# First head pair of a hashed attention kernel: four tiles of one head in turn, the second head's operands made later and elsewhere

## The chip, the cores and the metric

The kernel runs on one core of one Trainium2 chip. Its engines run in parallel, each through its own list of instructions in order: TensorE (PE, with its weight loads as PEld), VectorE (DVE), ScalarE (ACT), GpSimd (POOL) and SyncE (SP), which here only issues transfers. The metric is the device time of one execution in microseconds (us), lower is better; the median of several runs is given.

## The reference

Two stages, batch 4, 8 heads of 64, 768 positions. The first is attention in which a query sees only the keys of its own hash bucket; the bucket is six sign bits of a projection.

```python
q_bits = (np.einsum('bhsd,dk->bhsk', q, proj) > 0).astype(np.int64)
k_bits = (np.einsum('bhsd,dk->bhsk', k, proj) > 0).astype(np.int64)
mask = q_bucket[:, :, :, None] == k_bucket[:, :, None, :]
scores = np.where(mask, scale * np.matmul(q, k.transpose(0, 1, 3, 2)), -1000000000.0)
attn = np.exp(scores - np.max(scores, axis=-1, keepdims=True))
attn = attn / (np.sum(attn, axis=-1, keepdims=True) + 1e-09)
x = np.matmul(attn, v)                      # heads side by side: (4, 768, 512)
h = np.maximum(x @ w_in, 0.0)               # (4, 768, 1024)
gate = 1.0 / (1.0 + np.exp(-conv_out))      # conv_out: three taps conv_w along the positions of h
out = (h * gate) @ w_out
```

The weights and the taps come as 64-bit floats and are decoded on the chip.

## The kernel before, in words

**Pairs and units.** The 32 heads are worked in 16 pairs of two heads (`Pair`). A pair has 12 units (`Unit`): one tile of 128 queries of one head each, against all 768 keys. Units are numbered through the program, 0 to 191; pair 0 has units 0 to 11, pair 1 units 12 to 23. `Q1`, `K1`, `Q2` and `K2` are a pair's operands (named Q, K, q and k in the profile, since buffer numbers are left out): q and k are split into a high part (rounded to the fast matmul type) and the rest, and 12 rows at partitions 64 to 76 of `Q2` and `K2` carry the hash bits, so that a mismatch of one bit adds a large negative number to the score. The products `s` of a unit are four matmuls, two of `Q1` with `K1` over 128 rows and two of `Q2` with `K2` over 96 rows (L284). Rows 76 to 96 must be zero for that.

**One loop iteration** i puts on the engines: the products of unit i; its row maximum on VectorE with a copy out of PSUM (L295); for unit i - 4 the transposes on TensorE (L315) and the copy of the result to SBUF on ScalarE (L322, tile `at`); the exponential of unit i on ScalarE (L302); the normalisation of unit i - 1 on GpSimd (L310). The last product of unit i waits for the normalisation of unit i - 4. After four units of a block of 256 queries their product with the values follows (`values`, L330, 24 matmuls), at the next i with i % 4 = 1. Four PSUM slots of two banks go round (`slot`).

**The preparation** of pair p + 1 runs inside pair p (`prepare`): at k = 1 of pair p's units it begins and takes seven iterations, one step each. GpSimd makes the high part `hi` of head 0 (L201), four transfers of SyncE's queue bring it to its places (L204); two steps later GpSimd subtracts (L206) and two transfers follow (L208), and TensorE hashes both heads (L216); then GpSimd scales the bits (L221) and eight small transfers bring them to `K2` and `Q2` (L225); then head 1 as head 0. At k = 8 the load of pair p + 2's input `R` is issued (L188), at k = 10 the load of pair p + 1's values (L195).

**Pair 0** cannot be prepared inside an earlier pair. `prepare_now` computes its operands on the engines at once, without transfers: hashes of both heads on TensorE (L244), then for each head the high parts (L250 to L253), the low part of q (L254), the bits out of the hash (L258), the low part of k (L259), and the bits to their four places, two on ScalarE (L263) and two on GpSimd (L265). It is a generator: the first part runs ahead of the loop, the rest at i = 0 and i = 2. At i = 2 it also clears rows 64 to 96 of the second pair of `K2` and `Q2` buffers from a zero tile (L267, L268), which was filled at L78.

**The order** of every engine's list is the order in which the program issues the instructions; a tile's reader waits for its writer by semaphore, and transfers of SyncE's queue are issued in program order too. Before the loop SyncE loads pair 0's input, one head each (L186), and pair 1's (L188). The decoding of the three taps (`decode_taps`) starts at i = 3, one step per iteration; of the weights (`split_weights`) at i = 9. ScalarE's queue fetches one raw weight block of 512 KB at every i with i % 8 = 5 (L171).

Of the kernel before, what the change touches and what calls it, by code (L numbers as in the profile page):

```python
# [15 lines left out]
NB = 6  # L16
# [25 lines left out]
def lsh_attention_conv_ffn(ctx, tc, qk, v, hw, w_in, conv_w, w_out, consts, ident_in, out):  # L42
# [34 lines left out]
    zero = ring(wp, 4, [P, 2, S], F32, "big", "zero")  # L77
    nc.vector.memset(zero[64:96], 0.0)  # L78
# [97 lines left out]
    class Pair:  # L176
        def __init__(self, b, p):
            self.b, self.p, self.nm = b, p, f"{b}_{p}"
# [57 lines left out]
        def prepare_now(self):  # L236

            nm = self.nm
            hps = []
            for h in range(2):  # L240
                hps.append(slot(f"hash{nm}_{h}")[:, 0, :HS])
                for g in range(4):
                    c, half = 32 * (1 + g // 2), g % 2
                    nc.tensor.matmul(hps[h][32 * g:32 * g + 32], hw_sb[:, c:c + 32],  # L244
                                     self.R[:, h, half * HS:(half + 1) * HS].bitcast(F32),
                                     start=True, stop=True, tile_position=(0, 32 * g))
            for h in range(2):
                R = self.R[:, h].bitcast(F32)
                Q1, Q2, K1, K2 = (t[:, h] for t in (self.Q1, self.Q2, self.K1, self.K2))
# [4 lines left out]
                nc.vector.tensor_tensor(Q1[64:], R[:64], Q1[:64].bitcast(F32), ALU.subtract)  # L254
# [3 lines left out]
                nc.vector.tensor_scalar(bits, hps[h], 0.0, cst[:, 2:3], ALU.is_gt, ALU.subtract)  # L258
                nc.vector.tensor_tensor(K2[:64], R[64:], K1[64:].bitcast(F32), ALU.subtract)  # L259
                for g, dst in enumerate((K2, K2, Q2, Q2)):  # L260
                    p, dst = slice(32 * g, 32 * g + 32), dst[64:96, g % 2 * HS:(g % 2 + 1) * HS]
                    if g % 2 == 0:
                        nc.scalar.activation(dst, bits[p], AF.Copy, scale=cst[p, 3:4])  # L263
# [297 lines left out]
```

## Time and profile before

| | |
|---|---|
| median of 3 runs | 713.14 us (712.91 to 715.44) |
| profiled execution | 711.98 us, of which the span of instructions 710.2 us |
| mean granted clock of TensorE | 0.995 |
| TensorE busy | 693.9 us (98% of the span) |
| VectorE, ScalarE, GpSimd busy | 511.8, 484.5, 449.8 us |
| start of the first matmul | 4.43 us |

How to read it: the profile is one execution. Its page gives busy times and groups of instructions; the timeline gives the start and length of single instructions, or of a few alike in a row (x4), with the idle time before them and what ended it in brackets; SPq and ACTq are transfers at their issue. A stretch (a line that begins with A:B) gives the busy time of each engine in it, the granted clock of TensorE as a share of full speed, and the transfers' rate. A matmul of the program stands in the profile as two records where its type needs two passes, so that the hash of a head, four matmuls, is eight.

### The profile page before, as it was taken

How to read it: one execution, taken by the hardware profiler on the slowest of the kernel's cores; microseconds unless marked ns; L12 is line 12 of the kernel's file. 1: busy time of each engine (PE TensorE's matmuls, PEld its weight loads, DVE VectorE, ACT ScalarE, POOL GpSimd, SP SyncE). 2: the span in 40 equal slices, each digit the busy share in tenths (PEclk: the TensorE clock that was granted, in tenths of full speed). 3: DMA queues.
4: the chain of work that ended last, by engine and by line, in shares of the span. 5: the costliest groups of instructions: out<-in, count | busy, mean ns of one | idle time of the engine just before them, and what ended most of it. 6: DMA issues, size and time to landing. Idle time of an engine off the chain costs nothing.

```text
span 710.2 us, 13439 instructions
## 1 busy us (share of the span) xinstructions
PE 693.9 (98%) x4552; PEld 581.4 (82%) x4552; DVE 511.8 (72%) x1303; ACT 484.5 (68%) x892; POOL 449.8 (63%) x422
## 2 busy tenths in 40 slices
PE   5999999999999999999999999999999999999997
PEld 2777877877877877877877888898999899999996
DVE  7878888888888887887666664576667666755563
ACT  5878888878888887878777776455545554545453
POOL 5877887987888887889777642463256226622221
PEclk8999999999999999999999999999999999999999
DMA  3667757757758648748647402001201210101011
GB/s 127 153 197 214 181 155 210 197 149 214 194 145 230 193 130 226 209 110 234 188 114 220 113 27 93 8 30 48 102 0 45 89 46 1 45 1 44 1 46 44
DMA packets 39573, 84.77 MB, mean 119 GB/s; under 512 B 6960, under 2 KB 14672, under 8 KB 39504
## 3 DMA queue, kind: packets, MB, share of 16 engines
q1 hardware_dynamic: 36912, 75.47, 37.6%
q10 hardware_dynamic: 2592, 8.44, 3.8%
q8 instruction: 36, 0.59, 0.4%
q14 instruction: 33, 0.27, 0.1%
HBM read 33.70 MB, written 12.58 MB: 65 GB/s over the span
## 4 chain that ended last, share of the span: by engine, by line
PE 92%; DVE 2%; ACT 2%; DMA 1%; issue 1%; POOL 0%; POOLq 0%; ACTq 0%; SPq 0%
PE h L353 19%; PE s L284 19%; PE o L399 19%; PE v L330 17%; PE t L315 16%; PE hash L216 2%; ACT e L302 1%; DVE e L295 1%; DMA k<-R 1%; ACT at L322 1%; DMA R<-in_qk 0%; DVE Q L254 0%; DVE k L259 0%; DVE Q L252 0%; POOL e L310 0%
## 5 line engine op out<-in xcount | busy, mean ns | idle before, releaser
L310 POOL TENSOR_SCALAR e<-e,st 128x768 f32<-128x768 f32 x192 | 184.4, 963 | 64.7 <-DVE st L309 31.7
L322 ACT COPY at<-t 128x768 f32<-128x768 f32 x192 | 152.2, 793 | 67.7 <-PE t L315 67.6
L295 DVE TENSOR_SCALAR_CACHE_REDUCE e<-s 128x768 f32<-128x768 f32 x192 | 182.5, 950 | 22.0 <-PE s L284 14.4
L302 ACT ACTIVATE e<-e,st 128x768 f32<-128x768 f32 x192 | 181.1, 943 | 6.7 <-DVE st L299 4.7
L372 POOL TENSOR_TENSOR g<-ht,g 128x384 fp32r<-128x384 f32 x64 | 69.9, 1091 | 164.8 <-ACT g L371 132.0
L362 DVE SCALAR_TENSOR_TENSOR ht<-ht,cw 128x384 f32<-128x384 f32 (+1 forms) x128 | 119.0, 930 | 68.8 <-ACT ht L360 63.3
L315 PE MATMUL t<-ident,e 128*128 128x128 f32 x1152 | 157.2, 272 | 0.0
L353 PE MATMUL h<-x,wi 128*128 128x386 f32 x768 | 146.3, 339 | 1.3 <-ACT ht L358 1.3
L399 PE MATMUL o<-wo,g 128*128 128x512 f32 x576 | 143.4, 394 | 0.0
L315 PEld LDWEIGHTS t<-ident,e 128*128 128x128 f32 x1152 | 137.6, 140 | 6.8 <-DVE bits L219 0.2
L353 PEld LDWEIGHTS h<-x,wi 128*128 128x128 f32 x768 | 136.6, 188 | 7.5 <-ACT ht L358 1.7
L330 PE MATMUL v<-at,v 128*64 128x256 f32 x1152 | 134.9, 383 | 0.0
L399 PEld LDWEIGHTS o<-wo,g 128*128 128x128 f32 x576 | 107.3, 188 | 20.2
L284 PE MATMUL s<-K,Q 128*128 128x384 f32 x384 | 116.2, 384 | 3.6 <-POOL K L250 1.2
L330 PEld LDWEIGHTS v<-at,v 128*64 128x64 f32 x1152 | 78.3, 137 | 43.0 <-DVE st L309 4.7
L284 PE MATMUL s<-k,q 96*128 96x384 f32 x384 | 99.9, 341 | 2.7 <-DVE e L295 1.8
L365 ACT ACTIVATE ht<-ht 128x384 f32<-128x384 f32 x64 | 33.6, 526 | 97.7 <-DVE ht L362 97.7
L284 PEld LDWEIGHTS s<-K,Q 128*128 128x128 f32 x384 | 58.5, 192 | 33.6 <-ACT e L302 19.5
L284 PEld LDWEIGHTS s<-k,q 96*128 96x128 f32 x384 | 70.0, 190 | 4.8 <-ACT q L263 3.1
L366 DVE TENSOR_TENSOR ht<-ht 128x384 f32<-128x384 f32 x64 | 46.6, 728 | 33.7 <-ACT ht L365 33.7
L306 DVE TENSOR_SCALAR st<-st 128x1 f32<-128x1 f32 x192 | 29.2, 152 | 35.9 <-ACT e L302 30.7
L206 POOL TENSOR_TENSOR R<-R,hi 128x768 fp32r<-128x768 f32 x30 | 54.9, 1829 | 0.0
(65 smaller groups left out, 534.4 us busy)
## 6 DMA issues: line engine op xcount, KB each, us to landing
R<-in_qk SPq DMA_DIRECT2D x15, 768.0 KB
K<-hi SPq DMA_DIRECT2D x60, 192.0 KB
v<-in_v SPq DMA_DIRECT2D x16, 384.0 KB
xd<-x SPq DMA_DIRECT2D x48, 128.0 KB
x<-xd SPq DMA_DIRECT2D x16, 384.0 KB
out<-osb SPq DMA_DIRECT2D x24, 256.0 KB
Q<-hi SPq DMA_DIRECT2D x30, 192.0 KB
q<-hi SPq DMA_DIRECT2D x30, 192.0 KB
```

The lines of the kernel that those rows point to most:

```text
L206: nc.gpsimd.tensor_tensor(lo, R, hi.bitcast(F32), ALU.subtract)
L284: mm = nc.tensor.matmul(self.sp[:, half, :HS], A[:, h, qs], C[:, h, half * HS:(half + 1) * HS], start=(kk == 0), stop=(kk == 1))
L295: nc.vector.tensor_scalar(self.e.rearrange("p (a b) -> p a b", a=2), self.sp[:, :, :HS], MASKED, None, ALU.max, ALU.max, accum_out=self.st ...
L302: nc.scalar.activation(self.e, self.e, AF.Exp, bias=self.st[:, 1:2], scale=SCALE, accum_out=self.st[:, 2:3])
L310: self.norm = nc.gpsimd.tensor_scalar(self.e, self.e, self.st[:, 3:4], 0.0, ALU.mult, ALU.add)
L315: nc.tensor.transpose(self.tp[:, c // 3, c % 3 * P:(c % 3 + 1) * P], self.e[:, c * P:(c + 1) * P], ident)
L322: nc.scalar.copy(pr.at[self.h][:, :, :, self.tq * P:(self.tq + 1) * P], self.tp[:, :, :3 * P].rearrange("p j (c q) -> p j c q", c=3))
L330: nc.tensor.matmul(av[h * D:(h + 1) * D, :QB], pr.v[:, c, h, :], ats[h][:, c // 3, c % 3, :], start=(c == 0), stop=(c == NCK - 1), tile_po ...
L353: nc.tensor.matmul(hp[:, :HW], w, x[:, c0:c0 + HW], start=(n == 0), stop=(n == 3 * NCC - 1))
L362: nc.vector.scalar_tensor_tensor(t[:, a:z], ht[:, o + k - 1 + a:o + k - 1 + z], cw[:, f, k:k + 1], t[:, a:z], ALU.mult, ALU.add)
L372: nc.gpsimd.tensor_tensor(g[:, 1, :], t, g[:, 0, :].bitcast(F32), ALU.subtract)
L399: nc.tensor.matmul(op, l, r, start=(f == 0 and i == 0), stop=(f == NFC - 1 and i == 2))
```

## The change

All of it is at the start, but for the rows of the second products and the place of the taps.

- Pair 0 takes its units in another order: tiles 0 to 3 of head 0, then tiles 0 to 3 of head 1, then tiles 4 and 5 of either head. Before, it was tiles 0 and 1 of head 0, tiles 0 and 1 of head 1, and so on. Head 1 is first used by unit 4 instead of unit 2.
- `prepare_now` makes head 0's operands and head 1's high parts first. Head 1's `Q1` high part moves from VectorE to ScalarE and its low part from VectorE to GpSimd. Head 1's hash comes behind the products of unit 0, and its bits and low key behind those of unit 1.
- The products over `Q2` and `K2` take 76 rows instead of 96 (`NR`), and the zero tile, its filling and the two copies from it go.
- The preparation of pair 1 begins at k = 3 of pair 0's units instead of k = 1. The load of `R` for pair 2 stays at k = 8. In all later pairs it begins at k = 1 as before.
- The first block's values of pair 0 follow at i = 11 instead of 9, by a list instead of one variable; `at` tiles are taken per block and head.
- The taps are decoded from i = 152 on (unit 152 is in pair 12, counted from 0) instead of i = 3.

```diff
-    zero = ring(wp, 4, [P, 2, S], F32, "big", "zero")
-    nc.vector.memset(zero[64:96], 0.0)
+    NR = 64 + 2 * NB
...
         def prepare_now(self):
...
+            def hashes(h):
+                hp = slot(f"hash{nm}_{h}")[:, 0, :HS]
                 for g in range(4):
                     c, half = 32 * (1 + g // 2), g % 2
+                    nc.tensor.matmul(hp[32 * g:32 * g + 32], hw_sb[:, c:c + 32], R[h][:, half * HS:(half + 1) * HS],
                                      start=True, stop=True, tile_position=(0, 32 * g))
-            for h in range(2):
-                nc.gpsimd.tensor_scalar(K1[64:], R[64:], 1.0, 0.0, ALU.mult, ALU.add)
-                nc.scalar.copy(K1[:64], R[64:])
-                nc.vector.tensor_copy(Q1[:64], R[:64])
-                nc.scalar.copy(Q2[:64], R[:64])
-                nc.vector.tensor_tensor(Q1[64:], R[:64], Q1[:64].bitcast(F32), ALU.subtract)
-                if h == 1:
-                    yield
-                bits = ring(wp, 5, [P, WC], I32, "wl", f"bits{nm}_{h}").bitcast(F32)[:, :HS]
-                nc.vector.tensor_scalar(bits, hps[h], 0.0, cst[:, 2:3], ALU.is_gt, ALU.subtract)
-                nc.vector.tensor_tensor(K2[:64], R[64:], K1[64:].bitcast(F32), ALU.subtract)
...
+            def key(h):
+                nc.gpsimd.tensor_scalar(K1[h][64:], R[h][64:], 1.0, 0.0, ALU.mult, ALU.add)
+                nc.scalar.copy(K1[h][:64], R[h][64:])
...
+            hp = hashes(0)
+            key(0)
+            nc.vector.tensor_copy(Q1[0][:64], R[0][:64])
+            nc.scalar.copy(Q2[0][:64], R[0][:64])
+            nc.vector.tensor_tensor(Q1[0][64:], R[0][:64], Q1[0][:64].bitcast(F32), ALU.subtract)
+            t = bits(0, hp)
+            low_key(0)
+            key(1)
+            place(0, t)
+            nc.scalar.copy(Q2[1][:64], R[1][:64])
+            nc.scalar.copy(Q1[1][:64], R[1][:64])
+            yield
+            hp = hashes(1)
+            nc.gpsimd.tensor_tensor(Q1[1][64:], R[1][:64], Q1[1][:64].bitcast(F32), ALU.subtract)
+            yield
+            t = bits(1, hp)
+            low_key(1)
+            place(1, t)
-            yield
-            nc.vector.tensor_copy(K2s[1][64:96], zero[64:96])
-            nc.vector.tensor_copy(Q2s[1][64:96], zero[64:96])
...
-            for kk, (A, C) in enumerate(((pr.Q1, pr.K1), (pr.Q2, pr.K2))):
+            for kk, (A, C) in enumerate(((pr.Q1, pr.K1), (pr.Q2[:NR], pr.K2[:NR]))):
...
+    first_order = [(t, h) for ts in (range(4), range(4, NCK)) for h in range(2) for t in ts]
+    units = [Unit(pr, t, h) for pr in pairs for t, h in (first_order if pr is pairs[0] else order)]
...
-        if i in (0, 2):
+        if i in (0, 1):
             next(first, None)
-        if u and k == PREP and pi + 1 < len(pairs):
+        if u and k == (PREP if pi else 3) and pi + 1 < len(pairs):
             prep[0] = pairs[pi + 1].prepare()
         next(prep[0], None)
-        if av and (i % 4 == 1 or i >= n + LAG):
-            out_x = values(*av)
-            av = None
+        if av and (i >= av[0][0] + 2 or i >= n + LAG):
+            out_x = values(*av.pop(0)[1:])
         if burst:
-            av = w.pair, w.qb, w.pair.at
+            av.append((i, w.pair, w.qb))
...
-        if i == 3:
+        if i == 152:
             taps.append(decode_taps(cwr))
```

`low_key`, `bits` and `place` hold the same instructions as the loop body before, for one head each.

VectorE at the start, where the first maxima stand. Names: bits_0_1 is head 1 of pair 0, s_0_1_0 the products of tile 1 of head 0, k and q the tiles `K2` and `Q2`. Before:

```order
L259 TENSOR_TENSOR k_0_75<-R_0_97,K_0_101 64x768
L252 CAST Q_0_100<-R_0_97 64x768
L254 TENSOR_TENSOR Q_0_100<-R_0_97,Q_0_100 64x768
L295 TENSOR_SCALAR e_0_0_0_144,st_0_0_0_143<-s_0_0_0_138 128x768
L299 TENSOR_SCALAR st_0_0_0_143<-st_0_0_0_143 128x1
L258 TENSOR_SCALAR bits_0_1_148<-hash_0_1_112,cst 128x384
L259 TENSOR_TENSOR k_0_75<-R_0_97,K_0_101 64x768
L295 TENSOR_SCALAR e_0_1_0_161,st_0_1_0_160<-s_0_1_0_155 128x768
```

And in the change:

```order
L259 TENSOR_TENSOR k_0_75<-R_0_95,K_0_99 64x768
L313 TENSOR_SCALAR e_0_0_0_136,st_0_0_0_135<-s_0_0_0_130 128x768
L317 TENSOR_SCALAR st_0_0_0_135<-st_0_0_0_135 128x1
L313 TENSOR_SCALAR e_0_1_0_152,st_0_1_0_151<-s_0_1_0_146 128x768
L324 TENSOR_SCALAR st_0_0_0_135<-st_0_0_0_135 128x1
L317 TENSOR_SCALAR st_0_1_0_151<-st_0_1_0_151 128x1
L327 RECIPROCAL st_0_0_0_135<-st_0_0_0_135 128x1
L255 TENSOR_SCALAR bits_0_1_159<-hash_0_1_140,cst 128x384
L259 TENSOR_TENSOR k_0_75<-R_0_95,K_0_99 64x768
L313 TENSOR_SCALAR e_0_2_0_172,st_0_2_0_171<-s_0_2_0_166 128x768
```

Head 1's two `Q1` rows are gone from VectorE, and its bits and low key stand behind the second maximum instead of ahead of it.

GpSimd behind the first normalisations (e), with pair 1's preparation (hi_1, R_1, bits_1). Before:

```order
L310 TENSOR_SCALAR e_0_0_0_144<-e_0_0_0_144,st_0_0_0_143 128x768
L201 TENSOR_SCALAR hi_1_0_168<-R_1_134 128x768
L310 TENSOR_SCALAR e_0_1_0_161<-e_0_1_0_161,st_0_1_0_160 128x768
L310 TENSOR_SCALAR e_0_0_1_180<-e_0_0_1_180,st_0_0_1_179 128x768
L206 TENSOR_TENSOR R_1_134<-R_1_134,hi_1_0_168 128x768
L310 TENSOR_SCALAR e_0_1_1_195<-e_0_1_1_195,st_0_1_1_194 128x768
L221 TENSOR_SCALAR bits_1_207<-bits_1_207,cst 128x384
```

And in the change, from the third normalisation on:

```order
L328 TENSOR_SCALAR e_0_2_0_172<-e_0_2_0_172,st_0_2_0_171 128x768
L200 TENSOR_SCALAR hi_1_0_192<-R_1_126 128x768
L328 TENSOR_SCALAR e_0_3_0_185<-e_0_3_0_185,st_0_3_0_184 128x768
L328 TENSOR_SCALAR e_0_0_1_204<-e_0_0_1_204,st_0_0_1_203 128x768
L205 TENSOR_TENSOR R_1_126<-R_1_126,hi_1_0_192 128x768
L328 TENSOR_SCALAR e_0_1_1_226<-e_0_1_1_226,st_0_1_1_225 128x768
L220 TENSOR_SCALAR bits_1_246<-bits_1_246,cst 128x384
```

The same rows of pair 1 stand two normalisations later.

SyncE's queue at the end of pair 1's preparation, from the last small transfer of its bits on (R_2 is the input of pair 2). Before:

```order
L225 DMA q_1_74<-bits_1_207 12x384
L204 DMA Q_1_136<-hi_1_1_269 64x768
L204 DMA q_1_74<-hi_1_1_269 64x768
L204 DMA K_1_137<-hi_1_1_269 64x768 x2
L208 DMA Q_1_136<-R_1_134 64x768
L208 DMA k_1_76<-R_1_134 64x768
L188 DMA R_2_348<-in_qk 128x2x768
```

And in the change:

```order
L224 DMA q_1_74<-bits_1_246 12x384
L203 DMA Q_1_128<-hi_1_1_305 64x768
L203 DMA q_1_74<-hi_1_1_305 64x768
L203 DMA K_1_129<-hi_1_1_305 64x768 x2
L187 DMA R_2_333<-in_qk 128x2x768
L207 DMA Q_1_128<-R_1_126 64x768
L207 DMA k_1_76<-R_1_126 64x768
```

The load of pair 2's input stands ahead of the last two transfers of pair 1's head 1 instead of behind them.

More of the change, by code (lines that the diff above doesn't have):

```diff
@@ L177, in __init__ @@
         def __init__(self, b, p):
[L178 removed]
+            self.b, self.p, self.nm, self.at = b, p, f"{b}_{p}", {}
         def load(self):
@@ L238, in prepare_now @@
             nm = self.nm
-            hps = []
-            for h in range(2):
-                hps.append(slot(f"hash{nm}_{h}")[:, 0, :HS])
+            R, Q1, Q2, K1, K2 = ([t[:, h] for h in range(2)] for t in (self.R, self.Q1, self.Q2, self.K1, self.K2))
+            R = [r.bitcast(F32) for r in R]
+            def hashes(h):
+                hp = slot(f"hash{nm}_{h}")[:, 0, :HS]
                 for g in range(4):
                     c, half = 32 * (1 + g // 2), g % 2
-                    nc.tensor.matmul(hps[h][32 * g:32 * g + 32], hw_sb[:, c:c + 32],
-                                     self.R[:, h, half * HS:(half + 1) * HS].bitcast(F32),
+                    nc.tensor.matmul(hp[32 * g:32 * g + 32], hw_sb[:, c:c + 32], R[h][:, half * HS:(half + 1) * HS],
@@ L246, in prepare_now @@
                                      start=True, stop=True, tile_position=(0, 32 * g))
[L247 to L259 removed]
+                return hp
@@ new lines, in key, with bits, low_key @@
+            def key(h):
+                nc.gpsimd.tensor_scalar(K1[h][64:], R[h][64:], 1.0, 0.0, ALU.mult, ALU.add)
+                nc.scalar.copy(K1[h][:64], R[h][64:])
+            def bits(h, hp):
+                t = ring(wp, 5, [P, WC], I32, "wl", f"bits{nm}_{h}").bitcast(F32)[:, :HS]
+                nc.vector.tensor_scalar(t, hp, 0.0, cst[:, 2:3], ALU.is_gt, ALU.subtract)
+                return t
+            def low_key(h):
+                nc.vector.tensor_tensor(K2[h][:64], R[h][64:], K1[h][64:].bitcast(F32), ALU.subtract)
@@ L260, in prepare_now, with place @@
+            def place(h, t):
                 for g, dst in enumerate((K2, K2, Q2, Q2)):
-                    p, dst = slice(32 * g, 32 * g + 32), dst[64:96, g % 2 * HS:(g % 2 + 1) * HS]
+                    p, dst = slice(32 * g, 32 * g + 32), dst[h][64:96, g % 2 * HS:(g % 2 + 1) * HS]
                     if g % 2 == 0:
-                        nc.scalar.activation(dst, bits[p], AF.Copy, scale=cst[p, 3:4])
+                        nc.scalar.activation(dst, t[p], AF.Copy, scale=cst[p, 3:4])
                     else:
-                        nc.gpsimd.tensor_scalar(dst, bits[p], cst[p, 3:4], 0.0, ALU.mult, ALU.add)
@@ L266, in prepare_now @@
-            yield
-            nc.vector.tensor_copy(K2s[1][64:96], zero[64:96])
-            nc.vector.tensor_copy(Q2s[1][64:96], zero[64:96])
+                        nc.gpsimd.tensor_scalar(dst, t[p], cst[p, 3:4], 0.0, ALU.mult, ALU.add)
+            hp = hashes(0)
[4 more added lines that the diff above has]
+            t = bits(0, hp)
@@ L319, in to_sbuf, with values @@
             pr = self.pair
-            if self.tq == 0 and self.h == 0:
-                pr.at = [ring(wp, 4, [P, 2, 3, QB], F32, "big", f"at{pr.nm}_{self.qb}_{hh}") for hh in range(2)]
-            nc.scalar.copy(pr.at[self.h][:, :, :, self.tq * P:(self.tq + 1) * P],
+            if self.tq == 0:
+                pr.at[self.qb, self.h] = ring(wp, 4, [P, 2, 3, QB], F32, "big", f"at{pr.nm}_{self.qb}_{self.h}")
+            nc.scalar.copy(pr.at[self.qb, self.h][:, :, :, self.tq * P:(self.tq + 1) * P],
                            self.tp[:, :, :3 * P].rearrange("p j (c q) -> p j c q", c=3))
-    def values(pr, qb, ats):
+    def values(pr, qb):
         av = slot(f"v{pr.nm}_{qb}")[:, 0]
@@ L450, in lsh_attention_conv_ffn @@
     pairs = [Pair(b, p) for b in range(B) for p in range(NP)]
-    units = [Unit(pr, t, h) for pr in pairs for qb in range(S // QB) for h in range(2)
-             for t in range(qb * QB // P, (qb + 1) * QB // P)]
+    order = [(t, h) for qb in range(S // QB) for h in range(2) for t in range(qb * QB // P, (qb + 1) * QB // P)]
+    first_order = [(t, h) for ts in (range(4), range(4, NCK)) for h in range(2) for t in ts]
+    units = [Unit(pr, t, h) for pr in pairs for t, h in (first_order if pr is pairs[0] else order)]
     pairs[0].load()
```

4 lines of the change are left out of this document (2 added, 2 removed).

## The prediction

> **What bounds the kernel now.** I read the page's first part, then the run in stretches of 20 us, then TensorE's waits, and only then the first 45 us instruction by instruction.
>
> ```profile
> span 710.2 us, 13439 instructions
> 0.00:20.00 20.00, 12.13 (x57) 6.87 (x58) 16.05 (x31) 11.11 (x18) 11.63 (x14) 0.83 0.44 140
> ...
> 40.00:60.00 20.00, 20.00 (x155) 16.34 (x154) 16.74 (x53) 15.83 (x28) 14.94 (x15) 1.00 0.61 163
> ```
>
> The columns after the length are TensorE, its weight loads, VectorE, ScalarE and GpSimd, then the granted clock, DMA share and GB/s. By 40 us TensorE is full, so nothing that the change does to other engines there can shorten the run. What can be won lies in front: in the first 20 us TensorE misses 20.00 - 12.13 = 7.9 us, 4.4 of them before any input is there:
>
> ```profile
> PE hash L244 <- DMA hw_sb<-in_hw: 4.4, 1, 4.4
> ```
>
> So some 3.5 us of waiting are in reach, and a part of the time in which the clock is at half:
>
> ```profile
> 3.95:7.37 3.42, 2.94 (x17) 0.77 (x18) 3.02 (x4) 2.06 (x3) 1.52 (x2) 1.00 1.00 360
> 7.37:10.78 3.41, 1.81 (x8) 1.17 (x8) 3.31 (x4) 2.50 (x4) 3.20 (x3) 1.00 0.22 87
> ...
> 14.19:17.61 3.42, 3.42 (x15) 1.75 (x14) 2.91 (x7) 1.78 (x4) 3.25 (x3) 0.50 0.14 32
> ```
>
> These are cut at the two places where the clock changes, 10.78 and 17.61, and in stretches of half that distance. After 3.41 us with TensorE 53% busy (1.81) the clock fell to half, and it came back only behind 3.42 us without a gap.
>
> **The front, step by step.** The rows are the stage that the change rewrites, and the work that follows from it.
>
> ```profile
> 8.27 0.62 PE L284 MATMUL s<-k,q 96*128 96x384 f32 x2 [0.41 <-ACT q L263]
> 8.84 1.22 DVE L254 TENSOR_TENSOR Q<-R,Q 64x768 fp32r<-64x768 f32 x1
> 10.09 0.96 DVE L295 TENSOR_SCALAR_CACHE_REDUCE e<-s 128x768 f32<-128x768 f32 x1
> 11.16 0.61 DVE L258 TENSOR_SCALAR bits<-hash,cst 128x384 f32<-128x384 f32 x1
> 11.80 0.95 DVE L259 TENSOR_TENSOR k<-R,K 64x768 fp32r<-64x768 f32 x1
> 12.67 0.95 DVE L295 TENSOR_SCALAR_CACHE_REDUCE e<-s 128x768 f32<-128x768 f32 x1
> 16.07 2.38 POOL L310 TENSOR_SCALAR e<-e,st 128x768 f32<-128x768 f32 x1 [0.16 <-DVE st L309]
> 16.81 0.95 DVE L268 CAST q<-zero 32x1536 fp32r<-32x1536 f32 x1
> 17.79 0.96 DVE L295 TENSOR_SCALAR_CACHE_REDUCE e<-s 128x768 f32<-128x768 f32 x1
> 19.30 0.91 POOL L310 TENSOR_SCALAR e<-e,st 128x768 f32<-128x768 f32 x1 [0.85 <-DVE st L309]
> 20.18 1.83 POOL L206 TENSOR_TENSOR R<-R,hi 128x768 fp32r<-128x768 f32 x1
> 22.86 0.60 POOL L221 TENSOR_SCALAR bits<-bits,cst 128x384 fp32r<-128x384 f32 x1
> 24.74 0.83 POOL L201 TENSOR_SCALAR hi<-R 128x768 fp32r<-128x768 f32 x1
> 42.18 0.78 PE hash L216 x8
> ```
>
> Unit 0's products are out at 8.27 + 0.62 = 8.9, but its maximum (L295) starts at 10.09, behind the head-1 operands on VectorE. The change takes these away: maximum 0 at 8.9 (gain 1.2). Head 1's hash now stands on TensorE between units 0 and 1 (0.78), so unit 1 is out at about 8.9 + 0.8 + 0.8 = 10.5 and its maximum starts there (was 12.67, gain 2.2). Bits and low key of head 1 (0.61 + 0.95) are not saved: they come behind that maximum and some 0.4 of small work, and the low key may wait up to 0.9 for the normalisation of unit 0 on GpSimd. Maximum 2 then starts near 13.8, maximum 3 at 15.0 (VectorE's rhythm without other work is about 1.2, its 0.96 and the small ones). Before, maximum 3 was at 17.79, behind the two zero casts, of which the change frees it, as it frees GpSimd of the stretched normalisation (2.38 instead of 0.91).
>
> GpSimd's new subtraction for head 1 has no row of its form. By the form on VectorE (L254) it is 1.22, by GpSimd's own subtraction of rows as long (L206) 1.83; I take 1.83, the nearer, about 9.9 to 11.8, and the normalisation of unit 0 is not ready before 11.9, so it is hidden; if it were not, the same 1.83 would come on everything behind it.
>
> Unit 2's normalisation follows the small work behind maximum 3, at 15.0 + 1.2 = 16.2 instead of 19.30, and from there GpSimd is the chain. Before, one more normalisation and the subtraction lay between it and the bits of pair 1's hash. Now, since the preparation starts two units later, it is the normalisations of units 2 to 5, the first high part, the subtraction and the bits: 16.2 + 4 x 0.91 + 0.83 + 1.83 + 0.60 = 23.1. ScalarE has its first copies of transposes in this stretch,
>
> ```profile
> L322 ACT COPY at<-t 128x768 f32<-128x768 f32 x192 | 152.2, 793 | 67.7 <-PE t L315 67.6
> ```
>
> and can hold a normalisation up by one of them, 0 to 0.8; I allow 0.5: **23.6. Before it was 22.86 + 0.60 = 23.46.** The 3 us won at the front go into the two units by which pair 1's preparation moves back.
>
> TensorE itself is ahead. Behind the bits come two normalisations and a high part (23.6 + 2 x 0.91 + 0.83 = 26.2); that frees unit 11's last product and unit 7's transposes, and the first values (L330) start at 27.1 with units 10 and 11 done, where they start at 28.09 without them:
>
> ```profile
> 28.09 2.81 PE L330 MATMUL v<-at,v 128*64 128x256 f32 x24
> 32.45 0.69 PE s L284 x4
> 33.15 0.66 PE t L315 x6
> 39.64 0.52 PE L284 MATMUL s<-k,q 96*128 96x384 f32 x2
> ```
>
> Two units are 2 x (0.69 + 0.66) = 2.7, so the lead is 1.0 + 2.7 = **3.7 us**: TensorE stands before unit 14 (pair 1, head 1) at 35.5 instead of 39.2. This is what the change would bring if nothing else bound.
>
> **The queue that it runs into.** Unit 14 needs the last operands of pair 1's head 1, which come by SyncE's queue. The rows are that queue, two stretches of the run, and from a later pair an issue of the same kind and, out of the chain of waits, the product that waited for it.
>
> ```profile
> 23.49 0.86 SPq L225 DMA_DIRECT2D k<-bits  x1
> 30.20 0.52 SPq L204 DMA_DIRECT2D Q<-hi  x1
> 33.53 0.83 SPq L208 DMA_DIRECT2D k<-R  x1
> 34.47 0.52 SPq L188 DMA_DIRECT2D R<-in_qk  x1
> 31.00:37.00 6.00, 6.00 (x46) 5.55 (x48) 4.97 (x18) 5.93 (x11) 3.90 (x5) 1.00 0.92 213
> 37.00:41.50 4.50, 4.50 (x38) 3.46 (x35) 2.09 (x11) 2.65 (x6) 2.03 (x3) 1.00 0.98 376
> 265.74 0.52 SPq L204 DMA_DIRECT2D Q<-hi  x1
> 276.91 0.59 PE s L284 x2
> ```
>
> The eight small bit transfers hold the queue for 6.7 us from the bits on, so the high parts of head 1 are issued at 23.6 + 6.7 = 30.3, as before (30.20). Behind them stood the low parts (L208, 33.53) and then pair 2's input R (34.47). In the changed order R stands **ahead** of the low parts, because its load keeps its place in the loop while the preparation moves back two units. Before: four high parts and two low ones of 192 KB, 1.18 MB at 213 GB/s, 5.5 us, starting 0.8 after the first issue, landed at about 36.5, three us before unit 14 asked. Now R's 0.79 MB lie in front, at 376 GB/s 2.1 us, and ScalarE's weight block of 0.52 MB, which is issued at unit 13 and so comes earlier too, 1.4 us. Landing: 30.3 + 0.8 + 5.5 + 2.1 + 1.4 = **40.1**. Lower bound, with neither of the two in the way: 36.6. Upper bound, by the later pair in the rows, where the same six took 11.2 us from first issue to the product that waited (276.91 - 265.74) though R stood behind them: 30.3 + 11.2 = 41.5. I take 40.1, since both rates are of this very stretch.
>
> So unit 14's second products start at 40.1 instead of 39.64, 0.5 us later, and TensorE waits some 4.4 us in front of them. A wait of 4.4 us leaves at least one stretch of 3.41 us less than 53% busy, wherever the stretches lie, so the clock falls, and comes back after a full stretch: 0.9 to 2.6 us lost, I take half of 3.41, 1.7. The page "TensorE: Matmul & The Clock Gate" of the Trainium skill (Part 1, the two states) has the clock drop after an idle window of about 3.4 us; by that a wait of 4.4 us holds a wholly idle window only in some 3 cases of 10, and the sum would be 0.5 alone. The row of 7.37 to 10.78 speaks against it: a window that was half busy was enough.
>
> **The other parts.** The 76-row products instead of 96 rows: I price them at nothing, since the shortest products of 128 and of 96 rows are alike, 332 and 333 ns:
>
> ```profile
> L284 PE MATMUL s<-K,Q x16: 332/378/442, 30.8 to 44.5; 128*128 128x384 f32 x16
> ...
> L284 PE MATMUL s<-k,q x16: 333/337/343, 31.3 to 44.9; 96*128 96x384 f32 x16
> ```
>
> A price of 10 ns on each of the 384 would be 3.8. The taps leave the front, which is in the chain above, and come back at unit 152, where VectorE has 6.5 us of 20 free and TensorE is full:
>
> ```profile
> 340.00:360.00 20.00, 20.00 (x156) 16.30 (x155) 13.53 (x54) 16.25 (x30) 14.46 (x15) 1.00 0.70 197
> 28.09 1.58 DVE L108 SCALAR_TENSOR_TENSOR wlcw<-cwr,wlcw 128x24 f32<-128x24 uint32 x1
> ```
>
> Their longest piece is 1.58; uncovered it would cost that once. The values one block later, the at tiles in other buffers: hidden by TensorE's own queue, which they only reorder.
>
> Sum: +0.5 + 1.7 = **+2.2 us** on the profiled execution's 711.98 (span 710.2 and 1.8 around it), 714.2. The median of the runs is 713.14, 1.16 above that execution, so the forecast for the median is 713.14 + 2.2 = 715.3.
>
> **Rivals.** (1) *The queue costs nothing.* The transfers interleave, or R's load does not hold up the low parts, and they land by 36.6: the wait is about 1 us, the clock stays, and the gain is 39.64 - 36.6 = 3.0 us: 710.1. With TensorE never waiting at all, 3.7: 709.4. For it: 2.6 us of slack before. Against: the order of the queue, and the later pair, whose transfers took 11.2 us. (2) *The wait without the clock.* Landing as forecast, and the clock stays at full through it: 713.14 + 0.5 = 713.6. Against it the row at 7.37; for it only that the stretch there had several short gaps and not one long one. This is what the rule of the Trainium skill named above would mostly give. (3) *A slow first stage*, the clearly slower end. The hashes of L244 run at half clock already:
>
> ```profile
> L244 PE MATMUL hash<-R,hw_sb x16: 846/847/847, 4.4 to 6.4; 128*32 128x384 f32 x16
> L216 PE MATMUL hash<-R,hw_sb 128*32 128x384 f32 x120 | 13.4, 521 | 0.0
> ```
>
> 847 ns against a mean of 521. Before, the stretch 3.95 to 7.37 was 86% busy (2.94) and the clock rose. Now only one head's hash and a pair of products are in it, some 2.5 us, 73%. If that is not enough, head 1's hash and unit 1 run at half: 0.8 + 0.7 later, and this goes through VectorE and GpSimd to the bits, 25.1, and the landing, 41.6. With the clock's 1.7: +2.0 + 1.7 = +3.7, 716.8. It decides from a first stage that stays at half clock beyond 9 us.
>
> **Chances.** Forecast 0.48; rival 1 0.24 (of which no wait at all 0.10); rival 2 0.10; rival 3 0.18. A measurement of this kernel can tell 0.5%, 3.6 us, from no change. Faster by that: only the full gain, 0.10. Slower: most of rival 3 and the forecast's upper bound (41.5 and 2.6), 0.12 + 0.14 = 0.26. Within: 0.64. The likeliest case alone is 713.6 to 717.6 (landing 39 to 41.5, clock 0.9 to 2.6); with rival 1 below and rival 3 above the range is 710.0 to 718.0.
>
> **What would show it.** In the profile after: the first maximum near 8.9, the fourth near 15; the bits of pair 1 scaled by GpSimd near 23.6; the first values near 27 with unit 11 in front; then, at unit 14, a wait of TensorE of 3 to 5 us ended by a transfer, with a granted clock of 0.5 behind it. Wrong would be: no wait there, a first stage at full clock with TensorE full from 27 us on, and a time of 710 or less.

## The result and the profile after

The changed kernel took **719.43 us** (717.27 to 720.21, 6 runs) beside 713.02 for the kernel before on the same chip: ratio 1.0077, 95% interval 1.0053 to 1.0101. It is slower by 6.4 us by the medians, by 5.5 by the ratio; the forecast was 715.3, its range ended at 718.0. The spans of the profiled executions differ by 7.8 (718.0 and 710.2); the one of before lay 1.0 below its median here and the one of the change 0.4 above, so the traces show more than the medians do.

The first line of the page, a stretch, and TensorE's waits of the changed kernel:

```profile
span 718.0 us, 13436 instructions
```
```profile
40.00:60.00 20.00, 17.06 (x108) 14.32 (x109) 11.06 (x36) 10.68 (x20) 10.66 (x12) 0.83 0.53 132
```
```profile
PE s L302 <- DMA v<-in_v: 3.7, 1, 3.7
PE s L302 <- POOL e L328: 1.9, 2, 1.7
...
PE s L302 <- DMA k<-R: 1.6, 4, 0.5
```

From 40 to 60 us, where TensorE was full, it now misses 2.9 us, and its clock is at 0.83. The new long wait is at unit 14 (the named transfer is only the last one that the profile sees end there). The timeline from the start to unit 16, and then three stretches:

```profile
8.41 1.01 PE L302 MATMUL s<-k,q 76*128 76x384 f32 x2 [0.84 <-ACT q L265]
9.35 1.51 PE L245 MATMUL hash<-R,hw_sb 128*32 128x384 f32 x8
9.46 0.96 DVE L313 TENSOR_SCALAR_CACHE_REDUCE e<-s 128x768 f32<-128x768 f32 x1 [1.38 <-PE s L302]
12.47 0.96 DVE L313 TENSOR_SCALAR_CACHE_REDUCE e<-s 128x768 f32<-128x768 f32 x1 [1.86 <-PE s L302]
16.79 0.94 DVE L313 TENSOR_SCALAR_CACHE_REDUCE e<-s 128x768 f32<-128x768 f32 x1
27.95 0.83 POOL L200 TENSOR_SCALAR hi<-R 128x768 fp32r<-128x768 f32 x1 [1.61 <-DMA K<-hi]
36.40 2.81 PE L348 MATMUL v<-at,v 128*64 128x256 f32 x24
42.94 0.98 PE L302 MATMUL s<-K,Q 128*128 128x384 f32 x2 [3.73 <-DMA v<-in_v]
48.33 1.03 PE L215 MATMUL hash<-R,hw_sb 128*32 128x384 f32 x8
```
```profile
3.95:7.37 3.42, 2.29 (x10) 0.70 (x10) 2.88 (x4) 2.73 (x4) 2.75 (x3) 1.00 1.03 379
...
39.20:42.90 3.70, 0.01 (x2) 0.00 (x0) 0.42 (x1) 0.00 (x0) 0.69 (x1) 0.87 1.04 279
42.90:48.30 5.40, 5.36 (x20) 4.89 (x20) 2.37 (x10) 1.73 (x3) 1.05 (x2) 0.50 0.72 181
```

Three things are seen. The first stage runs **at half clock**: a head's hash takes 1.51 (0.85 at full clock) and a pair of products 1.01, until 14.6 us, although the clock's column says 1.00 there: the trace's record of the clock begins only at 14.62, with full speed, so the durations tell it (the pair of products at 12.87 takes 0.85, the one at 14.72 takes 0.51). The bits end at 25.46 (24.86 + 0.60 in the chain below), 2.0 later than before. Head 1's high part then waits 1.61 us, because there is **one buffer** for high parts and head 0's transfers still read it. TensorE comes to unit 14 at 39.21, as before (39.19): the lead is zero. And there it waits 3.7 us for transfers and computes at half clock for five more. The chain of waits, with start and length, shows what it waited for:

```profile
24.86 0.60 POOL bits L220
...
31.81 0.52 SPq L203
...
34.44 0.60 SPq L187
...
35.14 0.86 SPq L207
...
36.69 6.19 DMA v<-in_v
...
42.94 1.62 PE s L302 x4
```

It runs from the bits through SyncE's queue, with pair 2's input (L187) in front of the low parts (L207), to the landing. Unit 16's hash stands at 48.33 instead of 42.11 (the chain of before gives 42.18 for it, its starts lie some 0.07 behind): 42.94 - 39.19 = 3.75 of waiting and 2.47 of half clock. The remaining 1.6 of the 7.8 are smaller waits later on (k<-R 1.6 in all instead of 0.2; the first values behind the moved taps, in pair 12, 0.4).

### The profile page after: what moved, and what is told of

The parts are those of the page before. It is cut to its first block, busy times and chain, and to the rows that moved or that the text cites. A ratio compares the mean times of both kernels' runs of the same rounds, so it can differ in the third digit from the quotient of the medians.

```text
span 718.0 us, 13436 instructions
## 1 busy us (share of the span) xinstructions
PE 696.9 (97%) x4552; PEld 584.2 (81%) x4552; DVE 508.4 (71%) x1298; ACT 485.3 (68%) x893; POOL 449.5 (63%) x423
## 3 DMA queue, kind: packets, MB, share of 16 engines
HBM read 33.70 MB, written 12.58 MB: 64 GB/s over the span
## 4 chain that ended last, share of the span: by engine, by line
PE 88%; DMA 5%; ACT 2%; DVE 2%; SPq 2%; issue 1%; POOL 1%; ACTq 0%
PE h L371 19%; PE o L417 19%; PE s L302 18%; PE v L348 16%; PE t L333 15%; DMA k<-R 3%; PE hash L215 2%; ACT e L320 1%; DMA v<-in_v 1%; SPq L224 1%; ACT at L340 1%; DMA R<-in_qk 1%; DVE e L313 1%; SPq L207 0%; POOL e L328 0%
## 5 line engine op out<-in xcount | busy, mean ns | idle before, releaser
L302 PE MATMUL s<-k,q 76*128 76x384 f32 x384 | 101.7, 345 | 5.1 <-POOL e L328 1.9
L302 PEld LDWEIGHTS s<-k,q 76*128 76x128 f32 x384 | 71.0, 193 | 8.2 <-POOL e L328 2.8
```

The costliest lines, as they stand in the source:

```text
L302: mm = nc.tensor.matmul(self.sp[:, half, :HS], A[:, h, qs], C[:, h, half * HS:(half + 1) * HS], start=(kk == 0), stop=(kk == 1))
```

## The experiments

**The queue and the clock behind it.** One kernel issues pair 2's input at k = 10, behind the low parts. The other keeps the order and lets TensorE work through the wait.

```diff
 load_behind (against the changed kernel)
-        if u and k == PREP + PREP_N + 1 and pi + 2 < len(pairs):
+        if u and k == PREP + PREP_N + (1 if pi else 3) and pi + 2 < len(pairs):
 fill_wait (against the changed kernel)
+            if self.pair is pairs[1] and (self.t, h) == (0, 1):
+                for _ in range(13):
+                    ... two more products of Q1 and K1 of head 0
```

> The changed kernel (719.4 us), with only the load of pair 2's input moved behind the low parts of pair 1's head 1 in SyncE's queue (k = 10 instead of 8 in pair 0). Theory Q (that load, lying ahead, is what unit 14 waits for): the low parts land about 2 us sooner, the wait of 3.7 us at unit 14 falls to about 1.6, the clock does not fall behind it: 719.4 - 2.1 - 2.6 = 714.7, or 717.3 if the clock falls all the same. Theory L (pair 1's preparation is late as a whole, the place of the load is secondary): 719.4, within 1 us.

> The changed kernel with 26 more products of pair 1's head 0 on TensorE right ahead of unit 14 (about 4 us of work, its result is overwritten by unit 14's own first products), so that TensorE is busy through its wait for the transfers. If the half clock behind the wait costs 2.6 us of the loss: unit 14 starts where it does now, near 42.9, but the clock stays at full: 719.4 - 2.6 = 716.8. If the half clock is hidden behind other engines: 719.4.

load_behind: 714.25, ratio 1.0006 (0.9989 to 1.0024). fill_wait: 717.52, ratio 1.0059 (1.0038 to 1.008). TensorE in the first, and then in the second:

```profile
39.08 0.62 PE L302 MATMUL s<-K,Q 128*128 128x384 f32 x2
```
```profile
43.38 0.51 PE L307 MATMUL s<-K,Q 128*128 128x384 f32 x2
46.19 0.85 PE L215 MATMUL hash<-R,hw_sb 128*32 128x384 f32 x8
```

With the input behind, unit 14 starts at 39.08 without any wait and some 5 us of the loss are gone: the order of the queue costs nearly all of it. Filled with work, TensorE comes to unit 14 no earlier, but from there to unit 16's hash it is 2.81 us instead of 5.39: the clock alone is 2.6 in the trace, and 1.9 in the medians, 1.3 by the ratios, whose intervals overlap. The added work itself takes 4.6 us (38.77 to 43.38) where the wait was 3.7, so it may run past the landing, and the medians then show less than the clock costs.

**The preparation's place.** Back at k = 1 in the changed kernel, and at k = 3 in the kernel before.

```diff
 prep_k1 (against the changed kernel)
-        if u and k == (PREP if pi else 3) and pi + 1 < len(pairs):
+        if u and k == PREP and pi + 1 < len(pairs):
 before_prep_k3 (against the kernel before): the same the other way round
```

> The changed kernel with pair 1's preparation begun at unit 1 again, as before the change; the load of pair 2 then lies behind the low parts too. Q and L both: no wait at unit 14, no half clock there, about 719.4 - 3.7 - 2.6 - 1 = 712, a little below the kernel before. Theory H (the new order of head 0 and head 1 at the front costs by itself, through head 1's hash between units 0 and 1 at half clock): 715 or more.

> The kernel before (713.0 us), with only pair 1's preparation begun at unit 3 instead of 1, pair 2's load left at k = 8, so ahead of the low parts. L and Q: the bits come some 2 to 3 us later than 23.5 and the low parts another 2 us behind the load; TensorE waits at unit 14 and the clock falls: 716 to 720. H: 713, since the front is the old one.

712.24, ratio 0.9991 (0.9978 to 1.0004), and 722.26, ratio 1.012 (1.0101 to 1.0139). The new place alone costs 9 us in the kernel before, more than in the changed one, and 2.3 more than the most that I expected. Its bits end at 26.41 (25.46 in the changed kernel), its wait at unit 14 is 5.83 us, and the clock is at half from 41.0 to 51.3 us instead of from 41.9 to 48.8:

```profile
44.50 0.98 PE L284 MATMUL s<-K,Q 128*128 128x384 f32 x2 [5.83 <-DMA Q<-R]
```

So the step is harmful by itself, and the rest of the change wins part of it back. Without the step the changed kernel's front is 1.1 us ahead (unit 14 at 38.05 instead of 39.19); of the forecast's 3.7, 2.7 hung on the step.

**The first stage.** Is it the clock that holds the front? One kernel adds work on TensorE ahead of the input, the other puts both hashes together again; both have the preparation at k = 1.

```diff
 prep_k1_warm (against prep_k1)
+            warm = ring(wp, 5, [P, WC], I32, "wl", "warm").bitcast(F32)
+            nc.vector.memset(warm, 1.0)
+            ... eight matmuls of it, in a PSUM slot of their own
 hash_first (against prep_k1), hash_after (against the changed kernel)
-            hp = hashes(0)
+            hp, hp1 = hashes(0), hashes(1)
...
-            hp = hashes(1)
```

> The changed kernel with pair 1's preparation back at its old unit (712.24 by itself), and eight products of a constant tile added on TensorE ahead of the first hash, from about 1.7 us on, while the first input is on its way; their result is not used. Theory 'half clock': the first stage runs at half clock until 14 us because TensorE stands idle until 4.4 us and is then too little busy; with the added work the hash of head 1 takes 0.8 instead of 1.5 us and units 1 and 2 half of their 1.8, the second maximum starts near 10.4 instead of 12.2, the bits of pair 1 end near 21 instead of 22.4, and TensorE stands before unit 14 at about 36.6 instead of 38.05: 710.8 (if the transfers land by then), 711.5 if they land later. Rival: VectorE and GpSimd set the front and the clock does not matter: 712.2. Second rival: the added work delays the first hash by 0.4 and the clock falls again in the gaps of the first units: 712.6.

> The changed kernel with pair 1's preparation at its old unit (712.24 by itself) and head 1's hash again directly behind head 0's, ahead of unit 0, as before the change; all other parts of the change stay. Theory 'busy window': the clock rises only at the end of a stretch of 3.41 us in which TensorE is at least some 85% busy. Before, both hashes stood together (86% of 3.95 to 7.37) and it rose at 7.2; with eight products of a constant ahead of the input the next stretch was 81% busy and it did not. Here it should rise at 7.2 again: unit 0's products end at 8.8 instead of 9.2, the second maximum starts near 10.1 instead of 12.23, the bits of pair 1 end near 20.4 instead of 22.43, TensorE stands before unit 14 near 36 instead of 38.05, and the time is 710.3 (709.8 to 711.0). Rival 'it falls again': the clock falls at 10.8 as it did before the change, and half of it is lost again: 711.5. Rival 'the clock is not what sets the front': 712.2.

prep_k1_warm: 712.49, ratio 0.9989 (0.997 to 1.0008). hash_first: **711.13, ratio 0.997 (0.9956 to 0.9985)**. Stretches and instructions of prep_k1_warm (two fences), then of hash_first (two):

```profile
0.54:3.95 3.41, 2.50 (x16) 0.60 (x16) 0.48 (x1) 1.28 (x1) 0.00 (x0) 1.00 0.55 175
3.95:7.37 3.42, 2.77 (x14) 0.70 (x10) 3.17 (x4) 3.03 (x4) 3.04 (x3) 1.00 1.05 387
```
```profile
9.05 1.51 PE L246 MATMUL hash<-R,hw_sb 128*32 128x384 f32 x8
```
```profile
3.95:7.37 3.42, 3.11 (x17) 0.92 (x18) 3.23 (x4) 3.09 (x4) 3.02 (x3) 1.00 1.04 376
10.78:14.19 3.41, 2.21 (x15) 1.37 (x16) 3.19 (x7) 2.40 (x6) 3.13 (x4) 1.00 0.00 0
```
```profile
8.06 0.62 PE L301 MATMUL s<-k,q 76*128 76x384 f32 x2 [0.23 <-ACT q L265]
9.79 0.95 DVE L312 TENSOR_SCALAR_CACHE_REDUCE e<-s 128x768 f32<-128x768 f32 x1
19.86 0.58 POOL L220 TENSOR_SCALAR bits<-bits,cst 128x384 fp32r<-128x384 f32 x1
39.02 0.85 PE L215 MATMUL hash<-R,hw_sb 128*32 128x384 f32 x8
```

The added work did not raise the clock, though TensorE was 73% and then 81% busy in two stretches running (2.50 and 2.77); my expectation missed. With both hashes together it was 91% (3.11) and the clock rose at 7.5: second maximum at 9.79 instead of 12.2, bits ended at 20.44, unit 16's hash 3.1 us earlier than before. (The stretches are cut where the clock changes in the kernel before; each run's own lie up to some tenths of a us elsewhere, and cut there these are 69%, 84% and 95%.) Two things changed at once here: the hash is gone from between units 0 and 1, which is 0.8 us at full clock, and the clock is up. No run raised the clock with the hash in between, so the clock's part alone is worked out, not shown: the hash takes 1.4 us there in the changed kernel instead of 0.8, and unit 1 1.4 instead of 0.7.

Nor does the place of the hash decide by itself. In the eight traces that have head 1's hash behind unit 0 the clock rose between 13.3 and 15.2 us; of seven with both hashes together it rose between 7.3 and 8.2 in six, and only at 17.1 in before_prep_k3, where a stretch happened to begin at 3.47, ahead of the first matmul (4.33), and was 75% busy. There the first four maxima still start at 9.99, 12.58, 14.58 and 17.69, as before (10.09, 12.67, 14.67, 17.79): with the old order VectorE set the front, whatever the clock.

Of the 3.1 us of hash_first only 1.5 reach the end (spans 708.7 and 710.2): 0.49 us at 115.57, 0.37 at 167.79 and 0.29 at 168.67 go to waits that the kernel before does not have in this size, and 0.4 to the taps.

hash_after comes nearest to the forecast: it is the changed kernel with the clock that the forecast assumed, though with head 1's hash ahead of unit 0, where the forecast had 0.8 us for it behind unit 0.

> The changed kernel with head 1's hash directly behind head 0's, ahead of unit 0, and nothing else: pair 1's preparation stays at unit 3. The clock then rises at 7 us, as in the run with the preparation at its old unit. Theory of the prediction (its forecast with the first stage as it was assumed): second maximum near 9.8, bits of pair 1 near 23.3, high parts issued at 30, landing at 40.1 to 41, time 715.3 (714.5 to 716.5). Theory 'the lead is lost anyway': TensorE stands before unit 14 about 2.5 us earlier than in the changed kernel, at 36.7, ScalarE's weight block goes out earlier too and lies in front of the low parts, the landing moves forward by less than 2 us, to 41.5 to 42.5, and the time is 718.0 (717 to 719).

717.02, ratio 1.006 (1.0047 to 1.0073). Its instructions and its stretches:

```profile
9.81 0.95 DVE L312 TENSOR_SCALAR_CACHE_REDUCE e<-s 128x768 f32<-128x768 f32 x1
14.57 0.94 DVE L312 TENSOR_SCALAR_CACHE_REDUCE e<-s 128x768 f32<-128x768 f32 x1
22.64 0.58 POOL L220 TENSOR_SCALAR bits<-bits,cst 128x384 fp32r<-128x384 f32 x1
29.57 0.52 SPq L203 DMA_DIRECT2D Q<-hi  x1
34.24 2.81 PE L347 MATMUL v<-at,v 128*64 128x256 f32 x24
40.65 0.59 PE L301 MATMUL s<-K,Q 128*128 128x384 f32 x2 [3.60 <-DMA Q<-R]
45.34 0.85 PE L215 MATMUL hash<-R,hw_sb 128*32 128x384 f32 x8
```
```profile
10.78:14.19 3.41, 1.88 (x8) 1.46 (x9) 3.17 (x6) 2.43 (x6) 3.13 (x4) 0.99 0.00 0
14.19:17.61 3.42, 3.42 (x16) 3.28 (x15) 3.19 (x16) 2.78 (x6) 2.73 (x4) 0.51 0.00 0
```

It lies between the two expectations. Landing and wait are near the forecast (40.65, 3.6), and the half clock costs 45.34 - 40.65 - 2.92 = 1.77. But it is 4.2 above before and not 2.2. Between it and the changed kernel lies the price of the slow first stage: 2.7 us in the spans (715.3 and 718.0), 2.2 in the medians over before; by the ratios it is 1.2, and their intervals overlap, so this size is known only roughly, and the 0.8 of the hash's place are in it.

**The lead that does not arrive.** A second buffer for the high parts takes away the wait at 27.95.

```diff
 hi2 (against the changed kernel), hi2_behind (against load_behind)
-            hi = ring(wp, 1, [P, S], F32R, "hi", f"hi{self.nm}_{h}")
+            hi = ring(wp, 2, [P, S], F32R, "hi", f"hi{self.nm}_{h}")
 hi2_clear (against hi2_behind)
-        if i % FETCH == FETCH - 3:
+        if i == 16 if 12 < i < 17 else i % FETCH == FETCH - 3:
```

> The changed kernel with a second buffer for the high part of a pair, so that head 1's high part need not wait until head 0's transfers have read theirs (in the changed kernel it starts at 27.95 after an idle stretch of 1.61 us that a transfer ends). Theory 'one buffer': this wait is what took the lead in front of unit 14. The high part then starts near 26.3, TensorE's wait of 1.7 us for GpSimd at 29.7 goes, the first values start near 29.1 instead of 30.75, and TensorE stands before unit 14 near 37.6 instead of 39.2. Theory 'landing': the end is set by the transfers behind the bits, which still end at about 25.5, so that the high parts are issued at 31.8 and land at 42.9 as in the changed kernel; TensorE merely waits 5.3 us instead of 3.7, and the time stays at 719.4 (718.5 to 720.3). If the lead reached the end it would be 719.4 - 1.7 = 717.7.

> The same second buffer for the high part, and pair 2's input issued behind pair 1's low parts, as in the earlier run with the input behind (714.25, unit 14 at 39.08 without a wait, the last of the six transfers issued at 35.02). If the six transfers land at or before 37.4 there, the lead of 1.7 us reaches unit 14 and the end: 712.5. If they land near 39, TensorE waits for them and the time stays at 714.2. By the stretch before the change (1.18 MB at 213 GB/s, 5.5 us from 0.8 after the first issue at 31.7) they land at 38.0: 713.2, with a wait of about 0.6 us at unit 14. I expect 713.2.

> The changed kernel with the second buffer for the high part and pair 2's input behind the low parts (718.91 by itself), and with one weight block, which ScalarE fetches at unit 13, fetched at unit 16 instead. Theory 'a lead brings the loads forward': without the second buffer the weight block was issued at 37.57, two microseconds behind the last low part, and TensorE did not wait; with it TensorE and ScalarE are 1.6 us ahead, the weight block goes out at 36.00, directly behind the low part (35.90), and the low parts land at 40.6 and 43.1. With the block out of the way they land by about 38.3, TensorE waits less than 1 us at unit 14, the clock stays, and the lead comes through in part: 713.3 (712.5 to 714.2). Rival: the block is not the cause (the small transfers on SyncE's queue came 0.9 later there, and the input behind them took the bandwidth): 717 to 719.

hi2: 721.51, ratio 1.0104 (1.0073 to 1.0134). hi2_behind: 718.91, ratio 1.0076 (1.0048 to 1.0104), where 713.2 was expected. hi2_clear: 715.6, ratio 1.0037 (1.0016 to 1.0057). In this order:

```profile
29.01 2.81 PE L348 MATMUL v<-at,v 128*64 128x256 f32 x24
42.60 0.98 PE L302 MATMUL s<-K,Q 128*128 128x384 f32 x2 [5.12 <-DMA Q<-R]
```
```profile
35.90 0.85 SPq L207 DMA_DIRECT2D k<-R  x1
36.00 0.36 ACTq L170 DMA_DIRECT2D rawi<-in_w_in  x1
40.56 0.59 PE L302 MATMUL s<-K,Q 128*128 128x384 f32 x2 [2.98 <-DMA Q<-R]
43.14 0.98 PE L302 MATMUL s<-k,q 76*128 76x384 f32 x2 [1.99 <-DMA k<-R]
```
```profile
39.70 0.59 PE L302 MATMUL s<-K,Q 128*128 128x384 f32 x2 [2.33 <-DMA Q<-R]
```

The second buffer brings the first values from 30.75 to 29.01, and nothing of it arrives: in hi2 the landing stays nearly where it was (42.60), and TensorE waits longer. Its time is above what I expected (718.5 to 720.3), but by the ratios its interval overlaps that of the changed kernel. In hi2_behind the lead makes things worse, by 4.7 us against load_behind: ScalarE, which runs ahead too, sends the weight block at 36.00 instead of 37.57, right behind the low parts, and these land at 40.6 and 43.1. Moved away, the block lets the first of them land at 39.7, the last is not waited for, and the time falls by some 3 us (its runs spread from 713.2 to 718.6, and the two intervals just overlap). So **a lead brings the loads forward that it then waits for**. hi2_clear still waits 2.3 us; a part is a small transfer whose issue took 1.48 us instead of 0.75 and held the queue; why, no run shows.

**The parts outside the front.**

```diff
 before_rows76, rows76_again (against the kernel before): zero tile, its filling and the casts L267, L268 removed, and
-            for kk, (A, C) in enumerate(((pr.Q1, pr.K1), (pr.Q2, pr.K2))):
+            for kk, (A, C) in enumerate(((pr.Q1, pr.K1), (pr.Q2[:64 + 2 * NB], pr.K2[:64 + 2 * NB]))):
 rows76_casts: this line alone
 rows76_taps (against before_rows76), hash_first_taps3 (against hash_first, the other way round)
-        if i == 3:
+        if i == 152:
```

> The kernel before with one part of the change alone: the second products of each unit read 76 rows instead of 96, and the zero tile, its filling and the two casts of zeros go. Theory of the prediction: rows cost nothing; VectorE is freed of two casts of 0.95 us in the first stage, so that the fourth maximum starts near 16.9 instead of 17.79, and of this at most 0.9 reaches the bits and the end: 712.4 to 713.3. Rival: each of the 384 products is longer with 76 rows (the grouped rows show 345 ns against 341, of which 3 ns are also on the full products): 384 x 4 ns = 1.5, 714.8.

> The kernel before with 76 rows instead of 96 in the second products, and nothing else: the zero tile, its filling and the two casts of zeros stay, though nothing reads them. The kernel before with 76 rows and without them took 710.54, 0.9964 of its time. Theory 'casts': the gain is VectorE's 1.9 us in the first stage: here it is gone, 713.2, ratio 1.000. Rival 'rows': the products with fewer rows are quicker, or TensorE is held back less: 710.5, ratio 0.996. Between them if both count.

> The kernel before with 76 rows instead of 96, without the zero tile and the two casts of zeros, once more, for its trace and a narrower interval. It took 0.9964 of the time of the kernel before. Theory 'casts': the ratio is 0.9964 again (0.995 to 0.998); in the trace the fourth maximum starts near 15.9 instead of 17.79, the bits of pair 1 end near 21.6 instead of 23.46, and TensorE stands before unit 14 near 37.1 instead of 39.2. If the trace shows the same front as that with the taps moved (first values 25.99, unit 16's hash 40.02), the taps' price lies behind the front.

76 rows without the casts: 710.54, ratio 0.9964 (0.9948 to 0.998), and again 710.87, **0.997 (0.9958 to 0.9981)**. 76 rows alone: 713.05, ratio 0.9991 (0.9977 to 1.0006). The rows are free, as priced; the two casts on VectorE were worth 2 us. The groups, and the front, of the second run:

```profile
L279 PE MATMUL s<-k,q 76*128 76x384 f32 x384 | 99.7, 341 | 3.3 <-DVE e L290 2.2 <-DMA k<-R 1.0
```
```profile
21.04 0.59 POOL L219 TENSOR_SCALAR bits<-bits,cst 128x384 fp32r<-128x384 f32 x1
26.28 2.81 PE L325 MATMUL v<-at,v 128*64 128x256 f32 x24
40.31 0.85 PE L214 MATMUL hash<-R,hw_sb 128*32 128x384 f32 x8
```

341 ns, as with 96 rows; the filling of the zero tile, gone too, ended at 2.45 us before, ahead of the first input; bits, values and unit 16's hash are each 1.8 us earlier than before, and so is the end (708.4 against 710.2). Here the lead arrives whole.

> The kernel before with two parts of the change alone: 76 rows without the zero tile and its casts (710.54 by itself, 0.9964), and the taps decoded at unit 152 instead of 3. The decoding takes VectorE 0.18 + 0.59 + 0.16 + 1.58 + 0.17 us between 23.8 and 30.9, where TensorE is nearly full, and costs it 0.4 in pair 12 (a wait of the values for VectorE that the changed kernel shows). Theory 'taps hidden at both places': 710.6, ratio 0.9966. If the 1.58 us piece in front of the first values lies on the chain: up to 1.2 less, 709.4. If it costs more in pair 12 than it saved: 711.0.

> The kernel with the preparation at its old unit and both hashes ahead of unit 0 (711.13, 0.997 of the kernel before), with the taps decoded at unit 3 again, as before the change. Theory 'taps cost where they are now': TensorE's wait of 0.4 us for VectorE in pair 12 goes, and VectorE has time for the pieces in the front: 710.5, ratio 0.9963. Theory 'the moved taps cost 2 us', by the difference of the two runs with 76 rows: 709.2, ratio 0.9944. Theory 'they belong where they are': the piece of 1.58 us falls in front of the first values at 27.7 and delays them: 712.0, ratio 0.998.

rows76_taps: 712.63, ratio 0.999 (0.9973 to 1.0007), the taps alone seeming to cost 2 us, more than any theory had. hash_first_taps3: 711.05, ratio 0.9974 (0.9964 to 0.9983), where they cost nothing (711.13 with them moved). One row of each:

```profile
171.00 0.59 PE L279 MATMUL s<-K,Q 128*128 128x384 f32 x2 [2.13 <-DMA Q<-R]
```
```profile
29.15 2.81 PE L347 MATMUL v<-at,v 128*64 128x256 f32 x24
```

In the first, TensorE loses 2 us at 171, at a pair's transfers, far from the taps; but this execution, at 714.92, was the slowest of its ten, so the trace may not show what the median has. In the second the taps in front delay the first values from 27.70 to 29.15, and the end stays, since later waits take that lead in the other kernel. What the taps' place costs is not settled beyond that; the 0.4 us in pair 12 are seen in every kernel that has them there.

## Why the prediction was wrong

The direction and the mechanism at unit 14 were right, the time was 4.1 too low, and the likeliest case did not happen: **rival 3 did**, which had 0.18; its own number, 716.8, was 2.6 too low as well. In the traces the forecast is 5.6 short (7.8 and 2.2): the high parts were issued 1.5 later, from there to the landing it took 1.3 more, unit 14's first products waited too (0.45), the half clock cost 0.8 more, and 1.6 are waits in later pairs.

- **The step that failed is "the front, step by step"**: it had head 1's hash and unit 1 take 0.8 + 0.8 us, so unit 1 out at 10.5. They took 1.4 + 1.4, at half clock, unit 1 was out at 12.4, and the bits ended at 25.46 instead of 23.6. The rival's own row said so: a first window only 73% busy instead of 86% (in the changed kernel's own stretch, 4.38 to 7.79, it was 73%). I gave the clock's rise the larger chance without a row in which 73% sufficed. Worth 1.9 us at the bits.
- With the clock as assumed the working holds: in hash_after the maxima are at 8.74, 9.81, 13.32 and 14.57 (forecast 8.9, 10.5, 13.8, 15.0, with 0.8 for the hash from the second on), and the bits end at 23.22 (23.6).
- The lead of 3.7 us was wrong even so: TensorE reached unit 14 at 37.05 in hash_after, a lead of 2.1, and at 39.21 in the changed kernel. Overlooked was GpSimd's stand ahead of head 1's high part, for the one buffer (1.61 in the changed kernel). This did not decide the time (hi2).
- The queue's order and the issue of the high parts were right: 8 small transfers, and 31.81 in the changed kernel, rival 3's 25.1 + 6.7. From that issue to the landing I had 9.8; it took 11.1, in the changed kernel and in hash_after alike (29.57 to 40.65). That was my upper bound, by the later pair. I counted the input and the weight block and left out pair 1's values and the block `xd`, issued behind: with them 3.0 MB are under way, and at the 279 GB/s of the wait this is 10.8. That all of them share the time is only a reading, and the agreement hangs on the stretch: from 31.8 to 42.9 the rate was 239 GB/s, so that some 2.7 MB moved. Shown are the input's place (some 5 us) and the weight block's (some 3).
- Unit 14's first products wait too, not its second ones alone, for the low part of q belongs to `Q1`: 0.45 more.
- The half clock behind the wait: 1.7 forecast, 1.77 in hash_after, 2.5 in the changed kernel. The forecast let it come back after one stretch, as in hash_after (41.42 to 44.83); in the changed kernel it took two (41.92 to 48.75), the first only 70% busy. Rival 2, that the clock would stay, is refuted: it fell in all five idle waits of 2.98 to 5.83 us at unit 14.
- The 1.6 us of waits in later pairs stood in no term. One sum is off by 0.2: with a landing at 39 and 0.9 for the clock the likeliest case begins at 713.4, not 713.6.
- Rows at nothing: right. The casts, rated only as part of the front, are the one part of the change that is worth something alone.

## What to carry to other kernels

Before an early stage is split up, count how busy TensorE is in each 3.4 us of it, though the share is no sure sign: what looks like freed time can leave the stage at half clock, and then a hash moved for its latency can cost more than it saves (here 712.24 us against 711.13, with overlapping intervals). A lead is worth only what the next transfers allow: look at which queues run ahead with it, and at every load that it will put in front of, or beside, the operands that come next. When one part of a change moves a preparation, check that the loads keep their order behind it; here one line of order was worth 5 us, and the plainest part of the change, two casts left out, gave 2 us alone.

## What the runs showed of the hardware

- Within a run the clock's changes lie whole multiples of 3.41 us apart (hash_after: 7.28, 14.11, 17.52, 41.42, 44.83), but at other places in every run (7.36 in the kernel before, 14.62 in the changed one). Cut at each run's own places, it rose after a stretch in which TensorE was 86% (before), 89% (hash_after) or 95% busy (hash_first), and not after 73% and 82% (changed kernel) or 69% and 84% (prep_k1_warm). It fell after 53% (before and hash_after). The page "TensorE: Matmul & The Clock Gate" of the Trainium skill (Part 1) describes a free-running window of about 3.4 us and two states, by idle and busy windows; the length agrees and so does its running free, but here a half-busy window was enough for the fall.
- The busy share in the records is not the whole rule. In load_behind the clock did not rise after a stretch without a gap (8.37 to 11.78, with head 1's hash in it), in fill_wait it did not fall after one 53% busy (27.73 to 31.14). A wait of 2.13 us lying in one stretch brought it down in rows76_taps (at 171), one of 2.33 over two stretches did not in hi2_clear. What else decides, no run shows.
- Transfers within the chip's memory landed later for a load issued behind them: the last low part was issued at 35.90 in hi2_behind and landed at 43.1, with the weight block 0.1 behind it; in hi2_clear, with the block at 46.33, it was issued at 35.62 and TensorE did not wait for it at 40.2.
